# Retention, then a gated feed-forward: where q and k are turned, how the first tails are loaded, and in what pieces the exponents are issued

## The chip, the cores and the metric

The kernel runs on one core of a Trainium2 chip. Five engines work side by side, each through its own list of instructions in order: TensorE (PE in the profile; PEld are its weight loads), VectorE (DVE), ScalarE (ACT), GpSimd (POOL) and SyncE (SP), which here only issues transfers (DMAs). Engines wait for one another by semaphores. The metric is the device time of one execution in microseconds (us). The kernel before took 1175.51 us, the median of three runs (1174.72 to 1177.06).

## The reference

q, k and v are 8 x 8 x 576 x 64 (batch, heads, positions, head size). The feed-forward has 4608 tokens, 512 model columns and 1536 hidden columns. Everything is given as float64 or float32 and computed in float32.

```python
def _attn_ref(q, k, v) -> np.ndarray:
    ...
    scores = scale * np.matmul(q, k.transpose(0, 1, 3, 2))
    gamma = 1.0 - 2.0 ** (-5.0 - np.arange(H, dtype=np.float32))
    ...
    Dmat = np.where(rel >= 0, gamma[:, None, None] ** rel[None, :, :], 0.0)
    ret = scores * Dmat[None, :, :, :]
    return np.matmul(ret, v).astype(np.float32)

def _moe_ref(x, w_gate, w_val, w_out, rms_g) -> np.ndarray:
    rms = np.sqrt(np.mean(x * x, axis=-1, keepdims=True) + 1e-06)
    xn = x / rms * rms_g
    g = xn @ w_gate
    silu = g * (1.0 / (1.0 + np.exp(-g)))
    val = xn @ w_val
    return (silu * val @ w_out).astype(np.float32)
```

The retention's output, heads side by side, is the feed-forward's x.

## The kernel before, in words

**Jobs.** The retention is cut into 32 jobs: one batch and one pair of heads each. A job's 576 positions are nine chunks of 64: four full tiles of 128 positions and a tail of 64. `slot(j)` (line 387) issues on PE the values of job j-1 (L341), then the scores of job j (L270) and the states of its chunks (L290); on DVE it weighs the scores (`ret`, L302), adds the states up (`sums`, L319, with one copy at L317) and multiplies the finished output of job j-1 into x (L380), after PE's carried products (L360). A one-element memset on POOL (`tick`, L349) orders the carried products behind the values.

**Turns.** Scores need q and k with the head size on the partitions. For the first eight jobs `turn(j)` (line 209) does this with PE: 16 records turn_q, 4 turn_k, two for the tails (turn_t, L231) into one bank, and ACT copies them out (L228, L235). From job 8 on, `load_qk` (L142) loads q and k in 32 x 32 blocks into raw tiles, one buffer each, and `prepare(j)` turns them on DVE with two stream transposes (L241) and then scales v on ACT (L250). `following(j)` is `prepare_next(j)`, which prepares job j+1, and `load_next(j)`, which issues the loads of job j+2 on SP.

**Groups of tokens.** The 4608 tokens are 12 groups u of 384. Each has its norm: `norm_0` (squares on ACT, gathered on DVE), `norm_1` (three small products ms on PE, a power on POOL), `diagonals` (DVE, L453) and `norm_2` (a product rb on PE, four scalings of x on DVE, L466, and for u > 1 four differences, L477). Groups 0 and 1 are multiplied plainly: `up_plain` (L554) and `down` (L568). Groups 2 to 11 use seven products instead of eight: in `up(u, m, g)` (m = 0 gate, 1 val; g = 0 to 2) the products come in the order x, y, z, x, w, z, w into four PSUM banks (L497). After y comes the sum u2 = m1 + y on DVE, after z the sum u4 = u2 + z (both named u, L504). The second z product adds into the bank that u4 reads, so it waits for u4; the second w product waits in the same way for the sum c22 (in a gate group `h<-u,w`, in a val group `c<-u,w`). A generator yields after each of the seven. `across(u)` is the same for the output (L627), with 24 records a product. Five banks are shared by all of this. In `up_plain` PE runs ahead until five banks wait for ACT's Silu (L562) or DVE's product (L560).

**Order.** The program is written out by hand and each engine keeps the order of the trace. In the main loop (line 940), after group i of u, `behind(u, i)` puts a slot at certain i (`SLOTS`); it calls `slot(j)`, `prepare_next(j)` and, for i below 5, `load_next(j)`. During u = 2 one step of `combine_out` (DVE, L598) follows each yield.

**Weights.** They come as 64-bit floats in 18 chunks of 1 MB and are rounded on the chip: DVE takes the exponent bits (L745), ACT makes the new exponent in three pieces (L749, L750, L753, 1.15 us each), DVE makes the mantissa (L766, L771), puts in the sign (L775) and joins both (L783). L775 frees the words for the next load, which ACT issues. `weights(n)` issues n steps of this. `combine(m)` makes sums of weight blocks on POOL (L797).

**Start.** `start()` loads the first eight jobs on SP (`load_first`), and the tails of a batch with `load_tails`: all eight heads at once, three loads. Then come the eight jobs, `up_plain` for both groups, `down` for group 1 and for group 0 with slots 8 and 9 between, and the norm of group 2 among the products of `down(0, s)`.

Of the kernel before, what the change touches and what calls it, by code (L numbers as in the profile page):

```python
# [41 lines left out]
def kernel(  # L42
# [101 lines left out]

    def load_first(j):

# [34 lines left out]

    def load_tails(b, queues):


        room = w_up[1][:, 8:].rearrange("p b f -> p (b f)")
        for i, (nm, src) in enumerate((("qt", q), ("kt", k), ("vt", v))):
            t = room[:TAIL, (3 * b + i) * DM : (3 * b + i + 1) * DM]
            t = t.rearrange("p (h d) -> p h d", d=D)
            queues[i].dma_start(out=t, in_=src[b, :, NFULL * P :].rearrange("h p d -> p h d"))
            for hp in range(NHP):  # L190
                st[b * NHP + hp][nm] = t[:, 2 * hp : 2 * hp + 2]
# [17 lines left out]
    def turn(j):  # L209
# [19 lines left out]
        for i, nm in enumerate("qk"):  # L229
# [3 lines left out]
                identity=ident[:TAIL, :TAIL],  # L233
            )
            nc.scalar.copy(out=d[nm + "T"][:, NFULL * P :], in_=last[:, o])  # L235
    def prepare(j):

# [375 lines left out]
    def across(u):  # L613
# [27 lines left out]
        def result(row, col, a, ps):  # L641
            r = ps[:, :U]
            if a is not None:
                r = temp(f"c{row}{col}_{u}")
                add(r, a, ps)
            o = outs.tile([P, DM], F32, tag="o", name=f"o_{u}_{row}_{col}")[:, :U]
            nc.vector.transpose(out=o, in_=r)
            o = o.rearrange("p (d t r) -> p d t r", d=2, r=SQ)
            for d in range(2):
                for i in range(P // SQ):  # L650
                    c0 = row * DH + d * P + i * SQ
                    t0 = u * U + col * HU
                    queue = nc.scalar if u == NU - 1 and d else nc.sync
                    queue.dma_start(
                        out=out[t0 : t0 + HU, c0 : c0 + SQ].rearrange("(t c) r -> c t r", c=SQ),
                        in_=o[i * SQ : i * SQ + SQ, d],
                    )
# [80 lines left out]
    def exponent(i):  # L738

        if i not in words_of:  # L740
# [7 lines left out]
        )  # L748
        nc.scalar.activation(out=e.bitcast(F32), in_=e, func=AF.Relu, bias=least)  # L749
        nc.scalar.activation(  # L750
            out=e.bitcast(F32), in_=e.bitcast(F32), func=AF.Relu, bias=most, scale=-1.0
        )
        nc.scalar.activation(  # L753
            out=e, in_=e.bitcast(F32), func=AF.Relu, bias=top, scale=-(2.0**23)
        )
        exp_of[i] = e

    def mantissa(i):


        if i not in words_of:
# [69 lines left out]
    def start():  # L831
# [10 lines left out]
        nc.scalar.activation(out=tick, in_=mhalf[:1], func=AF.Silu)  # L842
        nc.vector.memset(ones, 1.0)
        first_places.update(find_places())
        for i in (1, 0, 2):
            table(i, nc.scalar)
        for j in range(2 * NHP):
            load_first(j)
            if j == 0:
                load_tails(0, (nc.scalar, nc.scalar, nc.sync))  # L850
            elif j == 1:
                table(3, nc.sync)
            elif j == 3:
                load_tails(1, (nc.sync,) * 3)
            load_chunks((0, 0, 1, 1, 2, 2, 2, 3)[j], nc.sync)
# [7 lines left out]
        for j in range(2 * NHP):  # L863
# [19 lines left out]
        load_kv(2 * NHP)  # L883
        for m, g in [(m, g) for g in range(NG) for m in range(2)]:
            for u in range(2):
                weights_to(4 * g + 2 * m + 1)
                for i, _ in enumerate(up_plain(u, m, g)):
                    if not (u or m or g):
# [98 lines left out]
```

## Time and profile before

| | |
|---|---|
| median of three runs | 1175.51 us |
| the profiled execution, by its own time | 1175.4 us |
| its span, first to last instruction | 1173.6 us |
| PE busy | 1134.3 us (97%) |
| DVE busy | 692.0 us (59%) |
| ACT busy | 248.7 us (21%) |
| bytes moved | 125.37 MB, 107 GB/s on the mean |
| first product of `up_plain` | 68.58 us |
| first product of `down` | 200.15 us |
| first product of `up(2)` | 267.01 us |

The main groups of instructions, from the list by line and shape: count, busy time, mean of one.

| line and what | count | busy us | mean ns |
|---|---|---|---|
| L241 turn of q, 128 x 576, DVE | 24 | 18.5 | 772 |
| L241 turn of k, 128 x 576, DVE | 24 | 17.6 | 735 |
| L504 sum u, 128 x 384, DVE | 120 | 66.0 | 546 to 554 |
| L749, L750, L753 exponent pieces, ACT | 18 each | 20.7 each | 1148 to 1149 |
| L562 Silu of `up_plain`, ACT | 24 | 10.9 | 477 to 484 |
| L235 tail copies, ACT | 16 | 3.4 | 212 to 218 |
| L647 output transposes, 128 x 384, DVE | 40 | 23.2 | 578 to 583 |

How to read it: a busy PE isn't PE at its peak, since ends of products are modelled. A wait is idle time of an engine just before an instruction, put down to what released it last. "issue" is a wait for nothing that the profile shows. Jobs 0 to 7 lie in the first 68 us, the plain products up to 264 us, and the rest repeats with small changes every three groups of tokens.

### The profile page before, as it was taken

The page shows a single profiled execution, that of the slowest core. Times are in us where ns is not written, and L with a number is a line of the kernel's source. Part 1 is how long each engine was busy: PE and PEld are TensorE (multiplying, and loading weights), DVE is VectorE, ACT ScalarE, POOL GpSimd, SP SyncE. Part 2 cuts the span into 40 slices and gives each one's busy share as a digit, 9 for nine tenths or more (in the row PEclk, how much of TensorE's full clock was granted, in tenths as well). Part 3 has the DMA queues.
Part 4 walks back from the last instruction along what each step waited for, and adds up shares of the span by engine and source line. Part 5 has one row for each costly group of instructions (what it writes and reads, how often), then busy time and mean ns, then how long its engine had stood idle before and what let it go on. Part 6 is the DMA issues. An engine that isn't in the chain of part 4 may idle for free.

```text
span 1173.6 us, 24291 instructions
## 1 busy us (share of the span) xinstructions
PE 1134.3 (97%) x10320; PEld 1024.2 (87%) x10320; DVE 692.0 (59%) x1410; ACT 248.7 (21%) x484; POOL 46.4 (4%) x74
## 2 busy tenths in 40 slices
PE   6689999998999999999999999999999999999998
PEld 5655555448999999999999999999999999999998
DVE  4688874018766675465675676356567566446352
ACT  5446641102111120121120211120220110120110
POOL 0000005410000000000000000000000000000000
PEclk9899999999999999999999999999999999999999
DMA  9744421422764546216426356306435412403304
GB/s 213 223 112 143 140 75 48 135 58 50 235 150 58 136 128 113 107 55 129 114 67 120 96 133 135 122 2 138 101 98 130 110 58 88 129 1 94 122 1 108
DMA packets 282364, 125.37 MB, mean 107 GB/s; under 512 B 257168, under 2 KB 264848, under 8 KB 282256
## 3 DMA queue, kind: packets, MB, share of 16 engines
q1 hardware_dynamic: 271584, 108.45, 37.2%
q10 hardware_dynamic: 10672, 15.38, 4.1%
q8 instruction: 81, 1.33, 0.5%
q14 instruction: 27, 0.22, 0.1%
HBM read 108.83 MB, written 14.94 MB: 105 GB/s over the span
## 4 chain that ended last, share of the span: by engine, by line
PE 83%; DVE 12%; issue 2%; DMA 2%; ACT 1%; DVEq 0%; SPq 0%; POOL 0%; POOLq 0%; ACTq 0%
PE z L497 12%; PE w L497 12%; PE x L497 10%; PE up L554 8%; PE xo L627 7%; PE wo L627 7%; PE zo L627 7%; PE out L568 5%; PE y L497 5%; PE yo L627 3%; DVE sum L319 3%; DVE x L380 2%; PE av L341 2%; PE s L270 2%; PE s L290 1%
## 5 line engine op out<-in xcount | busy, mean ns | idle before, releaser
L521 ACT COPY m<-x 128x384 f32<-128x384 f32 x60 | 28.8, 479 | 419.0 <-PE x L497 394.2
L497 PE MATMUL z<-x,w_gate 128*128 128x192 f32 x480 | 88.6, 328 | 6.6 <-DVE u L504 5.3
L497 PE MATMUL z<-x,w_val 128*128 128x192 f32 x480 | 88.6, 328 | 3.3 <-DVE u L504 3.3
L497 PE MATMUL x<-x,w_val 128*128 128x192 f32 x480 | 88.8, 328 | 0.0
L497 PE MATMUL x<-x,w_gate 128*128 128x192 f32 x480 | 88.5, 328 | 0.0
L497 PE MATMUL w<-sums,w_val 128*128 128x192 f32 x480 | 87.8, 326 | 0.0
L497 PE MATMUL w<-sums,w_gate 128*128 128x192 f32 x480 | 87.8, 326 | 0.0
L497 PEld LDWEIGHTS z<-x,w_gate 128*128 128x128 f32 x480 | 79.2, 190 | 8.9 <-DVE u L504 7.4
L497 PEld LDWEIGHTS z<-x,w_val 128*128 128x128 f32 x480 | 79.2, 190 | 5.7 <-DVE u L504 5.7
L627 PE MATMUL xo<-h,w_out 128*128 128x192 f32 x480 | 82.1, 328 | 0.0
L627 PE MATMUL wo<-h,w_out 128*128 128x192 f32 x480 | 81.3, 326 | 0.0
L497 PEld LDWEIGHTS x<-x,w_val 128*128 128x128 f32 x480 | 79.2, 190 | 0.6
L497 PEld LDWEIGHTS x<-x,w_gate 128*128 128x128 f32 x480 | 79.3, 190 | 0.5
L497 PEld LDWEIGHTS w<-sums,w_val 128*128 128x128 f32 x480 | 79.6, 190 | 0.0
L497 PEld LDWEIGHTS w<-sums,w_gate 128*128 128x128 f32 x480 | 79.6, 190 | 0.0
L627 PEld LDWEIGHTS xo<-h,w_out 128*128 128x128 f32 x480 | 78.1, 190 | 0.5
L627 PEld LDWEIGHTS wo<-h,w_out 128*128 128x128 f32 x480 | 78.5, 190 | 0.0
L504 DVE TENSOR_TENSOR u<-m,y 128x384 f32<-128x384 f32 x60 | 32.7, 546 | 77.5 <-PE y L497 77.5
L504 DVE TENSOR_TENSOR h<-u,w 128x384 f32<-128x384 f32 x60 | 33.2, 554 | 69.3 <-PE w L497 68.7
L302 DVE SCALAR_TENSOR_TENSOR ret<-s,causal 128x320 f32<-128x320 f32 x64 | 28.4, 484 | 67.6 <-PE last L290 41.7
L516 ACT ACTIVATE h<-h 128x384 f32<-128x384 f32 x90 | 47.1, 523 | 95.8 <-DVE h L504 95.8
L554 PE MATMUL up<-x,w_val 128*128 128x384 f32 x192 | 62.7, 487 | 2.4 <-ACT w_val L562 2.4
(151 smaller groups left out, 1779.2 us busy)
## 6 DMA issues: line engine op xcount, KB each, us to landing
w_out<-w_blocks SPq DMA_DIRECT2D x70, 768.0 KB, 5.3
out_dram<-o SPq DMA_DIRECT2D x304, 24.0 KB, 1.6
qraw<-in_q_dram SPq DMA_DIRECT2D x96, 72.0 KB, 2.6
kraw<-in_k_dram SPq DMA_DIRECT2D x96, 72.0 KB, 2.6
k<-in_k_dram SPq DMA_DIRECT2D x48, 128.0 KB, 3.0
v<-in_v_dram SPq DMA_DIRECT2D x48, 128.0 KB, 3.4
w_blocks<-w_out SPq DMA_DIRECT2D x7, 768.0 KB, 7.0
w_out<-in_moe_w_gate_dram ACTq DMA_DIRECT2D x4, 1024.0 KB, 5.2
```

Source lines behind the costliest of these rows:

```text
L270: nc.tensor.matmul(s[side(odd), e, i * L : i * L + L], lhsT=d["kT"][side(e), c * L : c * L + L], rhs=d["qT"][side(e), c * L : c * L + L], ...
L302: nc.vector.scalar_tensor_tensor(out=ret[:, e], in0=s[:, e, :SC].rearrange("p (c k) -> p c k", k=L), scalar=float(_gamma(H)[2 * hp + e] ** ...
L319: nc.vector.scalar_tensor_tensor(out=t[:, c], in0=t[:, c - 1], scalar=gc[:, hp : hp + 1], in1=part, op0=ALU.mult, op1=ALU.add,)
L341: mm = nc.tensor.matmul(av[odd][column(j, odd, e), i * L : i * L + L], lhsT=d["v"][side(odd), i, e] if c < NC - 1 else d["vt"][:, e], rhs= ...
L380: nc.vector.tensor_tensor(out=x[to, first - c0 // L :: 2], in0=av[odd][at, i * L : (i + n) * L].rearrange("p (c k) -> p c k", k=L), in1=g. ...
L497: nc.tensor.matmul(ps[:, i * HU : i * HU + HU], lhsT=w_up[m][:, 2 * blk + c, cut], rhs=t_of[u][blk][:, c], start=(start and i == c == 0), ...
L504: nc.vector.tensor_tensor(out=o, in0=a, in1=pairs_of(ps), op=ALU.add)
L516: nc.scalar.activation(out=o, in_=c, func=AF.Silu)
L521: nc.scalar.copy(out=s1, in_=pairs_of(x_))
L554: nc.tensor.matmul(ps[:, :U], lhsT=w_up[m][:, 4 * half + c, i * P : i * P + P], rhs=x_of[u][:, c], start=(c == 0), stop=(c == NHP - 1),)
L568: nc.tensor.matmul(ps[:, :DM], lhsT=h_of[u][:, f, s * P : s * P + P], rhs=w_out[:, f], start=(f == 0), stop=(f == NF - 1),)
L627: nc.tensor.matmul(ps[:, i * HU : i * HU + HU], lhsT=w_slots[:, k % 4, c, i * P : i * P + P], rhs=rhs[:, c], start=(start and i == c == 0) ...
```

## The change

- `load_tails` loads the tails of some heads only, one of q, k, v at a call, always on SP. For batch 0 the tails of heads 0 and 1 follow k and v of job 0, and those of heads 2 to 7 follow k and v of job 1; for batch 1 all eight heads follow k and v of job 4 (before, they came after job 3).
- `turn` issues both tail transposes, then both copies.
- Six products of a tile of ones into a bank of their own are issued on PE at the start.
- The three ACT pieces of an exponent go into a list `acts`; `act(1)` issues one of them at given points, and `act(chunk=i)` the rest of a chunk before L775 needs it.
- In the first jobs the last gather of group 0, its diagonals and its norm_2 are issued earlier; the norm of group 2 moves from `down(0, s)` to `down(1, s)`.
- `behind` no longer calls `prepare_next(j)`; it notes j in `turns`, and the turn is issued after the third yield of the next `up` (behind u2 and u4), or in `across` after its first product. `load_next(j)` stays where it was.
- In the last group of tokens each output transpose is done in two halves, and stores alternate between SP and ACT.

```diff
-    def load_first(j):
+    def load_first(j, tails):
...
+            for n in (0, 1) if nm == "k" else (2,):
+                load_tails(b, n, tails)
...
-    def load_tails(b, queues):
+    def load_tails(b, n, heads):
...
+        if heads:
+            room = w_up[1][:, 8:].rearrange("p b f -> p (b f)")
+            nm, src = (("qt", q), ("kt", k), ("vt", v))[n]
...
+            cut = slice(heads[0], heads[-1] + 1)
+            nc.sync.dma_start(
+                out=t[:, cut], in_=src[b, cut, NFULL * P :].rearrange("h p d -> p h d")
+            )
...
                 identity=ident[:TAIL, :TAIL],
             )
+        for i, nm in enumerate("qk"):
+            o = slice(i * TAIL, i * TAIL + TAIL)
             nc.scalar.copy(out=d[nm + "T"][:, NFULL * P :], in_=last[:, o])
...
+                if end:
+                    half = slice(d * HU, d * HU + HU)
+                    nc.vector.transpose(out=o[:, half], in_=r[:, half])
                 for i in range(P // SQ):
...
-                    queue = nc.scalar if u == NU - 1 and d else nc.sync
+                    queue = nc.scalar if end and i % 2 else nc.sync
...
+        f = e.bitcast(F32)
+        acts.extend((
+            (i, dict(out=f, in_=e, bias=least)), (i, dict(out=f, in_=f, bias=most, scale=-1.0)),
+            (i, dict(out=e, in_=f, bias=top, scale=-(2.0**23))),
+        ))
         exp_of[i] = e
+
+    acts = []
+
+    def act(n=0, chunk=-1):
+
+        while acts and (n > 0 or acts[0][0] <= chunk):
+            nc.scalar.activation(func=AF.Relu, **acts.pop(0)[1])
+            n -= 1
...
         yield
+        act(chunk=i)
         nc.vector.scalar_tensor_tensor(
             out=e, in0=hi, scalar=0x80000000, in1=e, op0=ALU.bitwise_and, op1=ALU.bitwise_or
         )
...
+        warm = bank("warm")
+        for _ in range(6):
+            nc.tensor.matmul(warm[:, :P], lhsT=ones, rhs=ones, start=True, stop=True)
...
-            load_first(j)
-            if j == 0:
-                load_tails(0, (nc.scalar, nc.scalar, nc.sync))
-            elif j == 1:
+            load_first(j, {0: range(2), 1: range(2, H), NHP: range(H)}.get(j))
+            if j == 1:
                 table(3, nc.sync)
-            elif j == 3:
-                load_tails(1, (nc.sync,) * 3)
...
+            act(1)
             if j == 5:
                 norm_1(0)
             elif j == 6:
+                norm_2(0)
+            weights((0, 1, 2, 2, 2, 2, 0, 0)[j])
+            if j == 4:
+                gather(*squares.pop())
+            elif j == 5:
                 diagonals(0)
-            weights((0, 1, 2, 2, 2, 2, 0, 0)[j])
-            if j == 6:
-                norm_2(0)
+            act(1)
...
                     weights(2)
+                    act(1)
                     if i == 1:
...
-                if u == 0:
+                if u == 1:
                     (norm_0, norm_1, norm_2)[s](2)
...
+    turns = []
+
     def behind(u, i):
...
             slot(j)
-            prepare_next(j)
+            turns.append(j)
...
-                for _ in up(u, i % 2, i // 2):
+                for n, _ in enumerate(up(u, i % 2, i // 2)):
                     next(made, None)
+                    if n == 2 and turns:
+                        prepare_next(turns.pop())
...
             for i, _ in enumerate(rest):
+                if i == 0 and turns:
+                    prepare_next(turns.pop())
```

More of the change, by code (lines that the diff above doesn't have):

```diff
@@ L180, in find_places @@
         }
-    def load_tails(b, queues):
-        room = w_up[1][:, 8:].rearrange("p b f -> p (b f)")
-        for i, (nm, src) in enumerate((("qt", q), ("kt", k), ("vt", v))):
-            t = room[:TAIL, (3 * b + i) * DM : (3 * b + i + 1) * DM]
-            t = t.rearrange("p (h d) -> p h d", d=D)
-            queues[i].dma_start(out=t, in_=src[b, :, NFULL * P :].rearrange("h p d -> p h d"))
-            for hp in range(NHP):
+    def load_tails(b, n, heads):
+        if heads:
+            room = w_up[1][:, 8:].rearrange("p b f -> p (b f)")
+            nm, src = (("qt", q), ("kt", k), ("vt", v))[n]
+            t = room[:TAIL, (3 * b + n) * DM : (3 * b + n + 1) * DM]
+            t = t.rearrange("p (h d) -> p h d", d=D)
+            cut = slice(heads[0], heads[-1] + 1)
+            nc.sync.dma_start(
+                out=t[:, cut], in_=src[b, cut, NFULL * P :].rearrange("h p d -> p h d")
+            )
+            for hp in range(heads[0] // 2, heads[-1] // 2 + 1):
                 st[b * NHP + hp][nm] = t[:, 2 * hp : 2 * hp + 2]
@@ L646, in result @@
             o = outs.tile([P, DM], F32, tag="o", name=f"o_{u}_{row}_{col}")[:, :U]
-            nc.vector.transpose(out=o, in_=r)
-            o = o.rearrange("p (d t r) -> p d t r", d=2, r=SQ)
+            end = u == NU - 1
+            if not end:
+                nc.vector.transpose(out=o, in_=r)
+            o_of = o.rearrange("p (d t r) -> p d t r", d=2, r=SQ)
             for d in range(2):
+                if end:
+                    half = slice(d * HU, d * HU + HU)
+                    nc.vector.transpose(out=o[:, half], in_=r[:, half])
                 for i in range(P // SQ):
@@ L652, in result @@
                     t0 = u * U + col * HU
-                    queue = nc.scalar if u == NU - 1 and d else nc.sync
+                    queue = nc.scalar if end and i % 2 else nc.sync
                     queue.dma_start(
                         out=out[t0 : t0 + HU, c0 : c0 + SQ].rearrange("(t c) r -> c t r", c=SQ),
-                        in_=o[i * SQ : i * SQ + SQ, d],
+                        in_=o_of[i * SQ : i * SQ + SQ, d],
                     )
@@ L748, in exponent @@
         )
[L749 to L755, printed above, removed]
-        exp_of[i] = e
+        f = e.bitcast(F32)
[3 more added lines that the diff above has]
+        ))
+        exp_of[i] = e
+    acts = []
[3 more added lines that the diff above has]
+            n -= 1
     def mantissa(i):
```

## The prediction

> **What bounds the kernel now.** First the page's header and its slices: TensorE (PE) is busy almost everywhere, and only the first three slices (29.3 us each), the tenth and the last are below nine tenths. The transfers are dense only in the first two.
>
> ```profile
> span 1173.6 us, 24291 instructions
> ...
> PE   6689999998999999999999999999999999999998
> ...
> DVE  4688874018766675465675676356567566446352
> ...
> DMA  9744421422764546216426356306435412403304
> ```
>
> So a gain must come out of PE's gaps: 1173.6 - 1134.3 = 39.3 us in all. The second view, what PE waited for (total, times, longest), names them:
>
> ```profile
> PE z L497 <- DVE u L504: 8.6, 15, 1.6
> PE s L290 <- issue: 4.6, 1, 4.6
> PE turn_q L223 <- DMA h<-in_q_dram: 3.9, 1, 3.9
> PE up L554 <- ACT w_val L562: 2.4, 1, 2.4
> PE av L360 <- issue: 2.3, 1, 2.3
> PE turn_t L231 <- ACT qT L235: 2.2, 5, 0.6
> PE turn_t L231 <- DMA w_val<-in_k_dram: 2.1, 1, 2.1
> PE turn_t L231 <- ACT qT L228: 1.9, 3, 1.6
> PE rb L464 <- DVE diag L453: 1.2, 1, 1.2
> PE z L497 <- DVE x L380: 1.2, 1, 1.2
> ```
>
> Third, the timeline of one slot in the steady part (start, us, engine). VectorE (DVE) turns q and k between the slot's sums and the sums u of the next group. The second z product must wait for the last u: PE's product before it began at 380.43, products stand 1.30 us apart, so z was due at 381.73.
>
> ```profile
> 379.73 0.77 DVE L241 STREAM_TRANSPOSE qT<-qraw 128x576 f32<-128x576 f32 x1
> ...
> 380.42 0.73 DVE L241 STREAM_TRANSPOSE kT<-kraw 128x576 f32<-128x576 f32 x1
> 380.43 1.46 PE L497 MATMUL w<-sums,w_val 128*128 128x192 f32 x8
> ...
> 381.08 0.52 DVE L504 TENSOR_TENSOR u<-m,y 128x384 f32<-128x384 f32 x1
> 381.70 0.56 DVE L504 TENSOR_TENSOR u<-u,z 128x384 f32<-128x384 f32 x1
> ...
> 382.31 1.57 PE L497 MATMUL z<-x,w_val 128*128 128x192 f32 x8 [0.41 <-DVE u L504]
> ```
>
> Last, windows over the first jobs (stretch, length, busy PE, weight loads, DVE, ACT, POOL, granted clock, DMA share, GB/s). Transfers fill the DMA engines, PE stands still for instructions from 45.2 to 49.8, and the clock falls to about 0.6 after each pause.
>
> ```profile
> 30.00:34.00 4.00, 4.00 (x102) 3.78 (x94) 2.37 (x8) 0.85 (x3) 0.00 (x0) 0.61 1.16 324
> ...
> 46.00:50.00 4.00, 0.18 (x12) 0.18 (x15) 0.00 (x0) 0.00 (x0) 0.00 (x0) 1.00 1.08 364
> 50.00:54.00 4.00, 4.00 (x67) 3.68 (x64) 3.37 (x13) 0.12 (x1) 0.00 (x0) 0.57 0.31 115
> ```
>
> **What the skill says.** "TensorE: Matmul & The Clock Gate", Part 1, says that the array runs at half clock until about 3.4 us of activity, and falls back after a pause. The trace agrees in effect: 16 turn_q records took 1.98 us at 12.64 and 1.09 us at 19.35, though its clock column shows 1.00 at both. The same page (Architectural detail) calls ScalarE (ACT) and DVE strict first-in first-out. The trace agrees: at 183.19 ACT's exponent had waited 8.0 us for DVE, and Silus of finished products stood behind it. "DMA: Bandwidth & Descriptors", Issuing engines are not separate DMA queues, says that loads from any queue share 16 engines. So moving the tails from ACT to SP moves issue time, not bandwidth; the share of 1.0 in the first 20 us fits. "Runtime: NRT & Kernel Launch", Instruction fetch mechanics, says that crossing a 256-instruction block is mostly hidden; here it isn't: 253 records ran from 40.4 to 45.2 between two stalls of 2.3 and 4.6 us.
>
> **The turns.** Twenty-one turns are deferred. Seven fall into the output products, 3.90 us each, where PE shows no wait: nothing gained or lost. Fourteen fall into an up group. Nothing leaves DVE: the turn (1.35 us of DVE's time) changes places with two u sums. Then z is free in time, and the next to be late is the second w product, which needs the sum c22 (`h<-u,w` or `c<-u,w`). That sum comes after the same set of work as before, so its end is unchanged. In a val group (8 of the 14) it ended at 383.18; w was due at 383.03 and started at 383.71. It can start at about 383.3: 0.4 us each, 3.2 in all. In a gate group (5) c22 ended at 572.83 against a due time of 572.82, before it w started at 573.63: 0.7 each, 3.5. The group at 299 also carries the steps of combine_out between the sums, c22 ends at 300.6 and w started at 300.79: 0.1. Sum 6.8. Bounds: all that is lost there now, 5 x 0.8 + 8 x 0.68 + 1.3 = 10.7 with restarts; 3.5 if only the gate groups gain. The four scalings of v on ACT (about 1.7 us) move between the copy m and the Silu; the 3.4 us that ACT idles there cover them. SP's loads of the next q and k (4 + 4 issues, 4.1 us, landing 2.6 us later) and of k, v, vt behind them wait for the turn, which ends about 1.2 us later. The tightest place is after the turn at 422.38: its reload of k is issued until 427.3, lands near 429.9, and the next turn comes at 436.55, 6.6 us later, and itself moves back; elsewhere over 10 us are left. Behind the loads on SP stand only weight fetches and stores.
>
> **Norm of group 2, earlier.** Before up(2), DVE does four scalings (2.20 us) and four differences (2.26) while PE wants the slot's and the group's sums: PE is busy 19.82 of 23 us in 267 to 290. Moved under down(1, .), all of it (squares on ACT, 3 ms products, POOL's power, diagonals) lies beside 31 us of PE work in which DVE is busy 2.45 of 33 us. The POOL power stands behind combine(0), which ended at 204.75, well before it is asked for at about 221; combine(1) behind it starts some 5 us later and was over at 234.9, 45 us before its use. What is late next: slot 9's turn, which is not deferred, as at 299 (1.0 us idle). So 3.2 idle become about 1.1, with 0.3 for restarts: 2.4. Bounds 1.3 and 3.3.
>
> **Exponents one at a time.** At 184.8 PE had filled its five banks, because two Silus waited at 186.62 behind three exponent pieces (3 x 1.15). With one piece between two Silus, the Silu starts when the first piece ends, 184.36: the 2.4 us go. DVE's L775 waits for the third piece up to 1 us longer; its product is needed at 200, ten us later. Bounds 1 and 2.4 us.
>
> **The first jobs.** The first tail k load (512 pieces, 4.5 us) held scores(0) to 10.17. With two heads' tails instead, and both tail transposes before their copies, the turn of job 0 could end near 7.2. But v of job 0 is now issued behind two more loads (about 0.6 us each, the price of a 32 KB vt load) and a wait, lands near 8.5, and takes 1.7 us to scale: states(0) start near 10.0, not 11.19: 1.2 us. The six warm products (12 records, about 1.5 us cold) run before 3.87, where PE waits for q anyway: at no cost there; they save anything from nothing to 3 us, as the clock may rise a few us sooner. Job 3: qT waits behind three exponents until 27.41, PE idles 1.56 and then runs 4 us at 0.61. Together 3.1. The tail copies: five waits of 0.4, of which I count 1.0 (the rest is DVE's). The norm of group 0: the diagonal is ready, 1.2, and 62 to 66 at 0.73 cost 1.1. Sum 7.6. Against it: v of jobs 3, 4 and 5 landed within about 0.5 us of its scaling (v of job 4 issued until 25.2 with 4.4 us to land, scaled at 29.05), and SP issues five loads more ahead of job 2 (2.7 us). What PE gains before 37 us is therefore partly given back to transfers and to the two instruction stalls, while jobs 6 and 7 have 4 and 8 us of slack. I take 6. Bounds: 10 (both stalls and all clock loss gone) and 0 (bound by transfers, stalls longer).
>
> **The end.** The last transpose is cut in two (0.39 us a half, from 0.58 for 384 and 0.77 for 576 columns), so the first stores start at 1169.46, not 1169.68. Each queue still has four issues (1.8 us): 0.2.
>
> **Sum.** 6.8 + 2.4 + 2.4 + 6.0 + 0.2 = 17.8 us. The profiled execution took 1175.4 us (its span of 1173.6 and 1.8 around it), almost the median of 1175.5. That gives **1157.6 us**.
>
> **Rivals.** (1) The start stays bound by transfers and instruction fetch, and val groups gain nothing: 0 + 3.6 + 2.4 + 2.4 + 0.2 = 8.6, hence 1166.8. For it: a DMA share of 0.76 to 1.31 in all windows from 8 to 50 us. Against it: jobs 6 and 7, and the waits on ACT and DVE, which are no transfers. Chance 0.25. (2) Slower: DVE stops at a deferred turn because its raw tile isn't there (q and k have one raw buffer, and its reload waits for this very turn), with five sums queued behind it and PE out of banks. Each us counts once per group. It decides from 0.8 us per group, (17.8 - 6.8) / 14, beyond what is lost now. At 1.5 us: 14 x 1.5 = 21 against 11 gained, so 1185.4. Against it stand the margins above. Chance 0.08. (3) The deferred turns don't move, because the loads traced ahead of them force the old order: 1175.4 - 11.0 = 1164.4. Chance 0.06, taken with the first.
>
> **How the numbers follow.** The forecast has 0.58, rivals 1 and 3 together 0.31, the slower one 0.08, no change 0.03. Faster by over 0.2% (what a measurement of this kernel can tell, 2.4 us): 0.89; within: 0.03; slower: 0.08. The forecast's own range is 1152 to 1163; with the bounds (low: 10 + 9 + 3.3 + 2.4 + 0.5 = 25.2, 1150.2; high: rival 1 and a little more) 1150 to 1168.
>
> **What would show it.** Right: no `z <- u` waits, at most 0.3 us at w in their place; z of up(2) waiting 1 us at most; no wait of up on the Silu; up's first product near 62 instead of 68.58. Wrong: waits of DVE on qraw or kraw, w waits over 0.8 us, or stalls of "issue" above 7 us in all before 70 us.

## The result, and the profile after

The kernel after takes 1155.86 us (median of 4 runs, 1155.05 to 1157.02); the kernel before, beside it, 1175.28 us (4 runs). The ratio is 0.9833, with a 95% interval of 0.9816 to 0.985: 19.6 us less, between 17.6 and 21.6. The profiled execution took 1157.02 us, its span is 1155.2 us.

The page of the kernel after, header and slices:

```profile
span 1155.2 us, 24332 instructions
...
PE   7899999999999999999999999999999999999998
...
DVE  3888864428676575465765775465576566445352
...
DMA  7945322322972656034345456306336403303304
```

Only two slices at the start and the last one are below nine tenths now; the dent in the tenth slice is gone. What PE waited for (total, times, longest), to be read against the list of the kernel before:

```profile
PE av L351 <- ACT qT L235: 3.4, 1, 3.4
PE s L280 <- ACT kT L235: 2.3, 2, 1.9
PE turn_t L238 <- ACT qT L235: 1.5, 3, 0.7
PE warm L868 <- DVE ones L865: 1.2, 1, 1.2
PE s L280 <- issue: 1.1, 2, 0.7
PE z L507 <- DVE u L514: 1.0, 1, 1.0
PE rb L474 <- DVE sum L329: 1.0, 1, 1.0
PE w L507 <- DVE h L514: 0.8, 1, 0.8
```

(Lines have moved by some ten: L507 is the old L497, L280 the old L270, L351 the old L341.) The 8.6 us of `z <- u` are down to one wait of 1.0, the wait of up for the Silu is no longer there, and the two stalls of "issue", 6.9 us, are short ones now. The first two lines are new.

The group with a deferred turn, in the timeline of the kernel after (start, us, engine):

```profile
366.69 1.46 PE L507 MATMUL x<-x,w_val 128*128 128x192 f32 x8
...
367.94 0.55 DVE L514 TENSOR_TENSOR u<-u,z 128x384 f32<-128x384 f32 x1
...
367.99 1.46 PE L507 MATMUL w<-sums,w_val 128*128 128x192 f32 x8
368.41 0.77 DVE L251 STREAM_TRANSPOSE qT<-qraw 128x576 f32<-128x576 f32 x1
369.11 0.73 DVE L251 STREAM_TRANSPOSE kT<-kraw 128x576 f32<-128x576 f32 x1
...
369.29 1.46 PE L507 MATMUL z<-x,w_val 128*128 128x192 f32 x8
...
370.21 0.54 DVE L514 TENSOR_TENSOR c<-u,w 128x384 f32<-128x384 f32 x1
...
370.80 1.57 PE L507 MATMUL w<-sums,w_val 128*128 128x192 f32 x8
```

Both u sums now end before the turn begins, and z starts 1.30 us after w, on time. The next w, due at 370.59, starts at 370.80 because c22 ends at 370.75: the 0.2 us that remain are at the place the prediction named.

Where the time went shows best by stages, whose limits are rows of the PE timelines. "First" is a product's start, the stages are differences (us). The upper rows are the two kernels, the others are the experiments below.

| kernel | first up | up to first down product | to first xo of u = 2 | to the end of the span |
|---|---|---|---|---|
| before | 68.58 | 131.6 | 134.8 | 838.6 |
| after | 62.39 | 128.9 | 131.3 | 832.7 |
| turns | 65.48 | 131.4 | 134.2 | 832.6 |
| norm | 67.70 | 131.1 | 132.2 | 838.7 |
| acts | 62.99 | 129.5 | 134.8 | 838.7 |
| acts_up | 68.56 | 129.5 | 134.8 | 838.6 |
| first | 68.64 | 131.4 | 134.8 | 839.1 |
| no_first | 63.31 | 129.3 | 131.3 | 832.5 |
| no_warm | 64.82 | 129.1 | 131.2 | 832.7 |
| short_warm | 61.26 | 128.9 | 131.2 | 832.7 |

So the 18.4 us of the spans are 6.2 in the first jobs, 2.7 in the plain up part, 3.5 up to u = 2's output and 5.9 after it.

But the first jobs have new waits too. The timeline there, ACT and PE:

```profile
13.02 0.51 ACT L260 ACTIVATE first_sums<-first_sums,gv 128x256 f32<-128x256 f32 x1 [4.15 <-DMA first_sums<-in_v_dram]
...
14.58 0.56 ACT L235 COPY qT<-turn_q 128x512 f32<-128x512 f32 x1
...
15.20 1.01 PE L351 MATMUL av<-ret,first_sums 64*64 64x64 f32 x26 [3.42 <-ACT qT L235]
```

Job 1's scaling of v stands ahead of job 1's turn copies on ACT. It waited 4.15 us for a v that SP issued at 8.79, behind the new tail loads, where before it did so at 7.27. The turned q and k lay ready in PSUM meanwhile, and av waited until their copy had freed its place.

### The profile page after: what moved, and what is told of

The parts are those of the page before. It is cut to its first block, busy times and chain, and to the rows that moved or that the text cites. A ratio compares the mean times of both kernels' runs of the same rounds, so it can differ in the third digit from the quotient of the medians.

```text
span 1155.2 us, 24332 instructions
## 1 busy us (share of the span) xinstructions
PE 1132.9 (98%) x10332; PEld 1025.7 (89%) x10332; DVE 696.4 (60%) x1414; ACT 246.4 (21%) x484; POOL 46.5 (4%) x74
## 3 DMA queue, kind: packets, MB, share of 16 engines
q8 instruction: 81, 1.33, 0.5%
## 4 chain that ended last, share of the span: by engine, by line
PE 91%; DVE 4%; SPq 2%; issue 1%; ACT 1%; DMA 1%; DVEq 0%; POOL 0%; POOLq 0%
PE w L507 13%; PE x L507 13%; PE z L507 13%; PE up L564 11%; PE xo L637 7%; PE wo L637 7%; PE zo L637 7%; PE y L507 6%; PE out L578 5%; PE yo L637 3%; PE av L351 2%; PE s L280 1%; PE s L300 1%; PE av L370 1%; SPq L161 1%; DVE sum L329 1%
## 5 line engine op out<-in xcount | busy, mean ns | idle before, releaser
L507 PE MATMUL w<-sums,w_val 128*128 128x192 f32 x480 | 88.6, 328 | 0.4
L507 PE MATMUL z<-x,w_gate 128*128 128x192 f32 x480 | 87.9, 326 | 1.0 <-DVE u L514 1.0
L507 PE MATMUL w<-sums,w_gate 128*128 128x192 f32 x480 | 88.0, 326 | 0.8 <-DVE h L514 0.8
L507 PE MATMUL x<-x,w_val 128*128 128x192 f32 x480 | 88.7, 328 | 0.0
L507 PE MATMUL x<-x,w_gate 128*128 128x192 f32 x480 | 88.5, 328 | 0.0
L507 PE MATMUL z<-x,w_val 128*128 128x192 f32 x480 | 87.8, 326 | 0.0
L507 PEld LDWEIGHTS w<-sums,w_val 128*128 128x128 f32 x480 | 79.2, 190 | 2.7 <-DVE c L514 2.7
L507 PEld LDWEIGHTS z<-x,w_gate 128*128 128x128 f32 x480 | 79.6, 190 | 1.3 <-DVE u L514 1.3
L507 PEld LDWEIGHTS w<-sums,w_gate 128*128 128x128 f32 x480 | 79.4, 190 | 1.3 <-DVE h L514 1.1
L507 PEld LDWEIGHTS x<-x,w_val 128*128 128x128 f32 x480 | 79.2, 190 | 0.6
L507 PEld LDWEIGHTS x<-x,w_gate 128*128 128x128 f32 x480 | 79.3, 190 | 0.5
L507 PEld LDWEIGHTS z<-x,w_val 128*128 128x128 f32 x480 | 79.6, 190 | 0.0
L564 PE MATMUL up<-x,w_gate 128*128 128x384 f32 x192 | 63.3, 488 | 0.9 <-DVE x L476 0.7
```

What stands on the lines that cost most here:

```text
L507: nc.tensor.matmul(ps[:, i * HU : i * HU + HU], lhsT=w_up[m][:, 2 * blk + c, cut], rhs=t_of[u][blk][:, c], start=(start and i == c == 0), ...
L564: nc.tensor.matmul(ps[:, :U], lhsT=w_up[m][:, 4 * half + c, i * P : i * P + P], rhs=x_of[u][:, c], start=(c == 0), stop=(c == NHP - 1),)
```

## Experiments: each part alone

Theory: the parts lie in different stages, so each is worth what its own waits were, and they add up. Rivals: the waits only move (turns, norm); the start is bound by transfers, so nothing that is done there counts.

The kernel before was run again beside each experiment; its medians there are 1175.8 to 1177.0 us. Each ratio is taken from all runs of the two kernels side by side and is not the quotient of the two medians; a gain in us below is (1 - ratio) times 1175.3. The stages come from one profiled execution each.

**turns**: the kernel before with the deferred turns alone.

```diff
-            prepare_next(j)
+            turns.append(j)
...
-                for _ in up(u, i % 2, i // 2):
+                for n, _ in enumerate(up(u, i % 2, i // 2)):
                     next(made, None)
+                    if n == 2 and turns:
+                        prepare_next(turns.pop())
...
             for i, _ in enumerate(rest):
+                if i == 0 and turns:
+                    prepare_next(turns.pop())
```

> The kernel before with the deferred turns alone. Theory (parts are separate, each worth what its own waits were): 6.5 us faster than before, near 1168.8, because fourteen up groups lose their z wait (0.66 on average) without a new wait at w; the output groups gain nothing; no z wait above 0.3 us after 300. Rival A (val groups gain nothing, w is late instead): 3.5 us faster, near 1171.8, with w waits of 0.5 us or more in val groups. Rival B (the turn is not the cause, the order of the sums is forced elsewhere): no change, z waits as before. First up product stays at 68.6 in both.

Measured: 1170.58 us, ratio 0.9934 (0.9916 to 0.9952), or 7.8 us (5.6 to 9.9). The stages put 6.0 us after u = 2 and 0.6 into u = 2. From 300 us on, the list of waits of PE has one line left (before: 6.0 us of `z <- u` in 13 waits, and this line):

```profile
PE av L360 <- POOL tick L349: 0.3, 1, 0.3
```

Both rivals fall. That its first up product came 3.1 us early although nothing was changed there is chance (the profiled execution, 1165.45 us, is the fastest of its six); see the instruction stalls below.

**norm**: the kernel before with one line changed, `if u == 0:` to `if u == 1:` at the norm of group 2.

> The kernel before with the norm of group 2 under the first output group alone. Theory: 2.4 us faster (1172.9), waits in 267 to 290 shrink from 3.2 to about 1.1 us, the output products of 200 to 267 unchanged. Rival (the norm's four scalings and differences displace DVE work under down that PE then waits for, or the slot behind it is late): less than 1 us, with new waits of s or ret between 230 and 260.

Measured: 1174.35 us, ratio 0.9973 (0.996 to 0.9986), or 3.2 us (1.6 to 4.7). The stage that holds it is 2.6 us shorter, and the one behind it stands (838.7 against 838.6). PE's waits from 267 to 290 us, 3.2 us in before, are down to one of z, 0.98 us. No wait of s or ret came up. The rival falls.

**acts** and **acts_up**: the exponents piece by piece; in acts everywhere, in acts_up in the plain up part alone.

```diff
-        nc.scalar.activation(out=e.bitcast(F32), in_=e, func=AF.Relu, bias=least)
...
+        acts.extend((
+            (i, dict(out=f, in_=e, bias=least)), (i, dict(out=f, in_=f, bias=most, scale=-1.0)),
+            (i, dict(out=e, in_=f, bias=top, scale=-(2.0**23))),
+        ))
         exp_of[i] = e
+        if not pieces:
+            act(3)
...
         gather(*squares.pop())
+        pieces.append(1)
         load_qk(2 * NHP)
```

The last three added lines are those of acts_up; acts has, in their place, the `act(1)` of the change behind the square and behind the weights of each first job.

> The kernel before with the exponents issued piece by piece alone (in the first jobs and in the plain up part). Theory: 2.4 us at the Silu of 184 to 187 and 1 to 3 us in the first jobs (the pause of job 3 and the slow clock after it): 3.4 to 5.4 us faster, near 1171. Rival (the first jobs are bound by transfers and instruction blocks, so only the Silu counts): 2.4 us faster, near 1172.9, first up product at 68.6 as before.

> The kernel before with the exponents issued piece by piece in the plain up part only; in the first jobs all three pieces follow each other as before. Theory (of the 8.5 us that all the pieces gave, 2.2 are the Silu's wait and the rest is made in the first jobs): 2.2 us faster than before, near 1173.5; first up product at 65.5 to 68.6, no wait of up on the Silu at 187. Rival (the pieces in the first jobs gave nothing and the earlier first up product of those runs was chance): 6 us or more faster.

Measured: acts 1168.49 us, ratio 0.9927 (0.9911 to 0.9942), or 8.6 us (6.8 to 10.5): more than either side had expected. acts_up 1173.8 us, ratio 0.9979 (0.9969 to 0.9989), or 2.5 us (1.3 to 3.6), with the up stage 2.1 us shorter and no Silu wait. The difference, 0.0052 or 6.1 us (about 4 to 8), is made by the pieces in the first jobs: 68.56 against 62.99 at the first up product.

**first**: the kernel before with the smaller tail loads on SP and both tails turned before their copies, without the warm products, exponents and norm as before.

```diff
-            load_first(j)
-            if j == 0:
-                load_tails(0, (nc.scalar, nc.scalar, nc.sync))
-            elif j == 1:
+            load_first(j, {0: range(2), 1: range(2, H), NHP: range(H)}.get(j))
+            if j == 1:
                 table(3, nc.sync)
-            elif j == 3:
-                load_tails(1, (nc.sync,) * 3)
```

> The kernel before with the smaller tail loads (all on SP, heads 0 and 1 first) and both tails turned before their copies; no warm products, the exponents and the norm of group 0 as before. Theory (job 0 earlier, later jobs give part of it back to v landing late): first scores before 8, a new wait near 15 for v of job 1, first up product 1 to 3 us earlier than 68.6, total 1 to 3 us faster. Rival A (it is the loads alone that make the start shorter): first up product near 63, 5 to 6 us faster. Rival B (transfer bound, tails in front of job 1 cost as much as they save): within 1 us of before.

Measured: 1177.02 us, ratio 0.9991 (0.9979 to 1.0002): 1.1 us, between 2.5 faster and 0.2 slower, which is rival B or the low end of the theory. The scores of job 0 do start at 7.62 instead of 10.17, and the first up product comes at 68.64, as before. Its waits show what took it back:

```profile
PE z L506 <- DVE u L513: 8.3, 14, 1.6
PE s L299 <- issue: 4.1, 1, 4.1
PE av L350 <- ACT qT L235: 4.1, 2, 2.1
```

The third line stands for two waits. The one of 2.0 us at 15.57 is the scaling of v ahead of the copies. In front of the one of 2.1 at 31.39 stood a scaling that waited 3.36 us for v, and behind it three exponents in a row, from 27.37 on, which the whole change issues one at a time; so the tails may be worth more in the whole change than alone. The second line is an instruction stall as before.

**no_first**: turns, norm and acts together, without the tail loads, the turn of both tails, the warm products, the earlier norm of group 0 and the halved last transpose.

> Deferred turns, norm of group 2 moved and exponents piece by piece, without the smaller tail loads, the turn of both tails at once, the warm products, the earlier norm of group 0 and the halved last transpose. Theory (the exponents alone made the start shorter, the tails are worth nothing): as fast as the whole change, 1155 to 1158, first up product at 62 to 64. Rival (the tails, warm products and norm of group 0 carry 3 us or more of the start once the exponents are out of the way): 1159 to 1162, first up product at 65 or later.

Measured: 1158.36 us (1156.7 to 1160.05), ratio 0.985 (0.9833 to 0.9867), or 17.6 us; first up product at 63.31. The three parts alone sum to 7.8 + 3.2 + 8.6 = 19.6, inside the interval of 15.6 to 19.6 at its edge. What it leaves out is worth 2.0 us by the ratios (2.5 by the medians), and the intervals overlap, so that it isn't told from nothing: between the theory and the rival, nearer the theory.

## Experiments: why the first jobs became shorter

In acts no transfer is moved in the program, and PE has the same instructions in the same order, so the gain of 5.6 us by the first up product can be followed from instruction to instruction. Job 3's wait of 1.56 us is gone, but in its place job 4's turn waits for ACT:

```profile
34.97 0.27 PE L231 MATMUL turn_t<-ident,w_val 64*128 64x64 f32 x1 [2.83 <-ACT qT L228]
...
45.81 0.39 PE L290 MATMUL s<-w_val,first_v 64*64 64x64 f32 x11 [0.96 <-issue]
...
46.10 1.11 PE L360 MATMUL av<-qT,sum 64*64 64x64 f32 x32
47.14 1.09 PE L223 MATMUL turn_q<-ident,h 128*64 128x128 f32 x16
```

That put acts 1.4 us behind (the carried products of L360 began at 38.77, in before at 37.35), and it caught up because the first instruction stall, 2.27 us at 40.41 in before, is missing. At 45 us acts is thus hardly ahead: the eleven records of `s` begin their stall at 44.85, those of the kernel before at 45.25, 0.4 us later. Then 3.6 us of the gain are the second stall's length, 0.96 against 4.57 us, and 1.6 us the pace of the two groups of products behind it, 1.96 and 1.85 us against 1.11 and 1.09. Together these are the 5.6. In the kernel before:

```profile
44.80 0.45 PE L290 MATMUL s<-w_val,first_v 64*64 64x64 f32 x14
49.82 0.39 PE L290 MATMUL s<-w_val,first_v 64*64 64x64 f32 x11 [4.57 <-issue]
...
50.10 1.96 PE L360 MATMUL av<-qT,sum 64*64 64x64 f32 x32
51.99 1.85 PE L223 MATMUL turn_q<-ident,h 128*64 128x128 f32 x16
```

Instructions come in packets of a queue of their own, among the data. In the view of the transfers from 47.0 to 47.5 us of the kernel before (queue, packets, MB, share of 16 engines):

```profile
DMA packets 148, 0.20 MB, mean 400 GB/s; under 512 B 42, under 2 KB 73, under 8 KB 147
...
q1 hardware_dynamic: 147, 0.18, 101.8%
q8 instruction: 1, 0.02, 12.8%
```

and from 43.0 to 43.5 us of acts:

```profile
DMA packets 455, 0.16 MB, mean 325 GB/s; under 512 B 410, under 2 KB 454, under 8 KB 454
...
q1 hardware_dynamic: 454, 0.15, 117.8%
q8 instruction: 1, 0.02, 15.8%
```

The page of the kernel before counts 81 packets of q8, 1.33 MB in all. PE and PEld have 20640 instructions, so one packet (0.02 MB) fits one block of about 255 of TensorE's instructions. In windows of half a microsecond, for all kernels in which this stall is at these same eleven records (the block that ends there begins with the records behind the first stall; in acts, which has no such stall, its begin is an estimate, 18 records into the group of 32 that starts at 38.77; the third weight chunk is a load of 1 MB that SP, in late_chunks ACT, issues near it):

| kernel | pieces in the first jobs | block begins | third chunk issued | q8 packet in | PE goes on at | stall |
|---|---|---|---|---|---|---|
| before | no | 40.41 | 40.65 | 47.0-47.5 | 49.82 | 4.57 |
| turns | no | 39.86 | 41.89 | 44.0-44.5 | 46.80 | 2.10 |
| norm | no | 39.18 | 39.22 | 46.5-47.0 | 49.65 | 4.84 |
| acts_up | no | 40.69 | 40.42 | 47.5-48.0 | 49.94 | 4.30 |
| first | no | 42.84 | 44.13 | 48.0-48.5 | 50.97 | 4.09 |
| late_chunks | no | 40.43 | 36.68 | 50.0-50.5 | 52.64 | 4.35 |
| acts | yes | 39.6 (estimate) | 41.94 | 43.0-43.5 | 45.81 | 0.96 |
| no_first | yes | 38.98 | 42.54 | 43.0-43.5 | 45.97 | 2.15 |
| no_warm | yes | 39.30 | 42.16 | 44.5-45.0 | 46.83 | 2.22 |

PE goes on some 2 to 3 us after the packet in every row, so the stall is a late packet. Before, turns, norm and acts_up are alike up to here, and their stalls still range from 2.1 to 4.8 us: a single profile of this start is uncertain by some 3 us. Over the rows, though, the stalls are 4.0 us on average without the pieces and 1.8 with them.

The third chunk sorts the rows better than the pieces do. Where it was issued before the block began or within 0.3 us of it (before, norm, acts_up, late_chunks), the packet passed 6.6 to 10.1 us after that begin; where it came 1.3 to 3.6 us behind it (the other five, turns among them), 3.4 to 5.7 us. This fits an instruction packet held up by data ahead of it: with the pieces SP issued this load at 41.9 to 42.5, in before at 40.65, although its line was not moved. But it is read from one profile of each kernel, and no run moved this load alone, so it isn't shown to be the cause.

**late_chunks** was to ask whether the weight chunks delay the packet.

```diff
-            load_chunks((0, 0, 1, 1, 2, 2, 2, 3)[j], nc.sync)
+            load_chunks((0, 0, 1, 1, 2, 2, 2, 2)[j], nc.sync)
...
-        load_chunks(4, nc.sync)
         turn(0)
...
+            if j > 5:
+                load_chunks(j - 3)
             if j:
                 u, c = divmod(j - 1, NHP)
```

> The kernel before with the loads of the weight chunks 3 and 4 (1 MB each) issued on ACT in the loop of jobs 6 and 7 instead of on SP with the jobs' loads. Theory (TensorE's instruction packets come late behind data packets; the second instruction stall ended about 2.5 us after its packet, and the packet came 4.4 to 6.8 us after the block before it began): with less data in flight at 40 to 50 us the second stall falls from 2.1 to 4.8 us to at most 1 us, first up product 2 to 4 us earlier, 2 to 4 us faster. Rival (q, k and v of the last jobs already fill the queues, chunks 3 and 4 come after the stall): stall and time unchanged within 1 us.

Measured: 1181.03 us, ratio 1.0034 (1.0021 to 1.0047), 4.0 us slower, and the stall stays (4.35). Neither theory nor rival expected that, and the theory wasn't put to the test, because the edit did not defer the loads: the rounding steps of jobs 2 to 5 ask for chunks five ahead and now found chunks 3 and 4 still to be issued, so ACT issued them itself at 36.68 and 37.50, and the chunk that it had issued at 37.25 followed at 40.92. The timeline of ACT:

```profile
36.68 0.40 ACTq L729 DMA_DIRECT2D w_out<-in_moe_w_val_dram  x1
...
37.50 0.41 ACTq L729 DMA_DIRECT2D w_gate<-in_moe_w_val_dram  x1
...
40.92 0.37 ACTq L729 DMA_DIRECT2D w_out<-in_moe_w_gate_dram  x1
41.34 1.15 ACT L749 ACTIVATE w_gate<-w_gate,least 128x1024 f32<-128x1024 uint32 x1 [2.77 <-DVE sum L319]
```

The three exponents behind it began at 41.34 instead of 37.85, the next turn copies stood behind them, and PE waited 3.1 us for ACT. So this run doesn't tell which data the packet waits for. It did the opposite of what was meant: both chunks went out earlier than in before (40.65 and 45.98), and the packet came later than in any other row. It shows again what three exponents in a row cost when a job's copies come due.

**no_warm** and **short_warm**: the kernel after without the six warm products, and with one column instead of 128 in each.

```diff
-            nc.tensor.matmul(warm[:, :P], lhsT=ones, rhs=ones, start=True, stop=True)
+            nc.tensor.matmul(warm[:, :1], lhsT=ones, rhs=ones[:, :1], start=True, stop=True)
```

> The kernel after without the six warm products. Theory (turn_q runs at 1.98 us for 16 records with and without them, and TensorE waits for v of job 1 at 15 us anyway): within 1 us of after, 1155 to 1157; turn_k and the first scores at about 1.35 instead of 0.8 us, the wait at 15 us shorter by as much. Rival (the early clock carries through the first jobs): 2 us or more slower than after, first up product at 64 or later.

> The kernel after with the six warm products cut to one column each: as many instructions ahead of the first turn, so the 256-instruction blocks end at the same places, but about 0.8 us of work instead of 2.9. Theory (the warm products are worth 2 to 3 us because they shift the places where TensorE waits for its next instructions): as after, 1155 to 1157, the instruction pauses at the same instructions as there, turn_k and first scores back at about 1.1 and 0.8 to 1.35. Rival (they are worth it through the clock, 7 to 10 us at full speed instead of half): as without them, 1158.5 to 1160.5, although the pauses stay where after has them.

Measured: no_warm 1159.64 us (1156.78 to 1162.01), ratio 0.9856 (0.9837 to 0.9876); short_warm 1156.53 us (1155.84 to 1158.12), ratio 0.9842 (0.9829 to 0.9856); after 0.9833 (0.9816 to 0.985). By the ratios the six products are worth 2.7 us (3.8 by the medians), against my expectation of under 1, and the short ones 1.6 (3.1); the three intervals overlap, so that neither is told from nothing. What the traces do show is that the earlier pace of after is lost again by 15 us. PE's timeline of after:

```profile
5.96 0.79 PE L224 MATMUL turn_k<-ident,first_k 128*128 128x128 f32 x4
...
15.20 1.01 PE L351 MATMUL av<-ret,first_sums 64*64 64x64 f32 x26 [3.42 <-ACT qT L235]
```

and of short_warm:

```profile
5.80 1.12 PE L224 MATMUL turn_k<-ident,first_k 128*128 128x128 f32 x4
...
15.38 1.01 PE L351 MATMUL av<-ret,first_sums 64*64 64x64 f32 x26 [3.08 <-ACT qT L235]
...
40.41 1.02 PE L370 MATMUL av<-qT,sum 64*64 64x64 f32 x26 [3.24 <-issue]
```

In short_warm turn_k took 1.12 us, as without warm products, and both kernels then wait for v of job 1 at 15 us. (The short products spanned 2.7 us, not the 0.8 that I expected, and the long ones 2.9; the two kernels differ less in this time than in the pace of turn_k behind it.) With twelve records more in front, the pauses for instructions fall on other records than in no_warm, as the theory says; but they aren't always shorter, as the 3.24 at 40.41 shows, where after has none. If the products are worth anything, shifted block ends are the explanation that is left; they aren't shown to be the cause.

## Experiments: a faster version

**scale_later** takes up the new wait at 15 us: v of a job is scaled behind the same job's copies.

```diff
         scale_v(0)
-        scale_v(1)
...
                 turn(j + 1)
+                scale_v(j + 1)
             if squares:
                 gather(*squares.pop())
-            if j + 2 < 2 * NHP:
-                scale_v(j + 2)
```

**sums_first** takes up z at 265.9 and w at 289.0, **best2** does both in a milder form.

```diff
         slot(9)
-        following(9)
+        turns.append(9)
+        load_next(9)
...
-                    next(made, None)
+                    if n not in (1, 2):
+                        next(made, None)
```

In best2 the last two lines are `for _ in range((2, 0, 0, 0, 2, 2, 2)[n]): next(made, None)`.

> The kernel after with v of a job scaled on ACT after the turn copies of the same job instead of one job ahead. Theory (the copies of job 1 stood 3.4 us, those of job 4 1.9 us, behind a scaling that waited for v): both waits go, first up product 2 to 4 us earlier than 62.4, total 2 to 4 us faster than after, near 1152. Rival A (the states then wait for the scaling, 1.7 us a job, which values and scores do not cover): waits of s on ACT in several jobs, no gain or slower. Rival B (the freed time goes to instruction stalls): no gain, longer stalls of issue.

> The kernel after with the turn of slot 9 deferred into the first group of u = 2 too, and the 24 differences of w_out spread over four or five groups and kept from between the u sums. Theory: the waits of z at 265.9 (1.0) and w at 289.0 (0.8) go, 1.5 to 2 us faster than after, near 1154. Rival (the differences then come late for across, or the turn is late for slot 10): xo of u = 2 waits on SP's fetch or DVE, no gain.

> The kernel after with v of a job scaled behind the turn copies of the same job, the turn of slot 9 deferred into the first group of u = 2, and two of the 24 differences of w_out at a time issued after the copy m and after c22, done in the fourth group as before. Theory: no wait of xo on the fetch (8.9 us when the differences ended in the fifth group), z at 266 and w at 289 together 1.8 shorter, the start 0 to 1.5 us shorter: 1 to 3 us faster than after, 1153 to 1155. Rival (two differences at a time make the slot's sums late instead): waits of w or x on DVE of 1 us or more between 266 and 300, no gain.

Measured: scale_later 1155.4 us, ratio 0.982 (0.9804 to 0.9836); sums_first 1168.54 us, ratio 0.9931 (0.9917 to 0.9946); best2 1155.2 us, ratio 0.9819 (0.9801 to 0.9837).

In scale_later the two waits are gone and the first up product comes at 60.87, 1.5 us earlier than in after; a stall of 3.43 us for instructions at 37.83 and waits of s for the scaling (1.4 us in three) took the rest, so that both rivals hold in part. sums_first does remove z's wait, but gave back far more; its list of waits begins

```profile
PE xo L637 <- DMA w_out<-w_blocks: 8.9, 1, 8.9
```

The differences end two groups later, SP can fetch the blocks of w_out only from 324.26 instead of 304.88, and the output products wait for them: the rival's case. best2 keeps the old end of the differences and has no such wait; in u = 2 the timeline of PE has

```profile
264.94 1.57 PE L507 MATMUL w<-sums,w_gate 128*128 128x192 f32 x8 [0.22 <-DVE h L514]
280.94 1.54 PE L507 MATMUL z<-x,w_gate 128*128 128x192 f32 x8 [0.29 <-DVE x L390]
285.72 1.57 PE L507 MATMUL z<-x,w_gate 128*128 128x192 f32 x8 [0.65 <-DVE u L514]
287.51 1.57 PE L507 MATMUL w<-sums,w_gate 128*128 128x192 f32 x8 [0.22 <-DVE h L514]
```

1.4 us in four waits for 1.8 in two, and the stage is 131.7 against 131.3 us: nothing won. Neither of the two quicker kernels is told from after by its interval.

## Why the prediction was right, point by point

The forecast of 17.8 us met 19.6 (17.6 to 21.6). Term by term:

- **Turns, 6.8.** Right in size and in mechanism: 6.6 us by the stages of turns, 7.8 (5.6 to 9.9) by its time. The next to be late is w, by 0.2 us, behind c22, as worked out (0.3). In one group it was more: w waits 0.85 us at 288.97, which by the letter is over the 0.8 that the prediction named as a sign of being wrong. It is the group (299 in before) in which the steps of combine_out stand between the sums; there z had waited 1.01 us, so its gain is near the 0.1 that was counted. The loads that the later turn pushes back cost nothing: no turn is listed as waiting for its raw tile (an output's transpose is, once, 1.5 us beside a load of kraw, with no wait of PE behind it), so rival 2 had no place to start from, and rival 3 falls with turns.
- **Norm of group 2, 2.4.** Right: 2.6 by its stage, 3.2 (1.6 to 4.7) by time. Slot 9's turn is what is late next, with 0.97 us at 265.91 (predicted 1.1). One reading was off, with nothing hanging on it: combine(1) was over at 237.6 in before, not at 234.9.
- **The Silu, 2.4.** Right: 2.1 by its stage, 2.5 (1.3 to 3.6) by time.
- **The first jobs, 6.0.** The sum was right (6.2 at the first up product), its terms were not, so that the hit is in part luck. Job 3's exponents, put at 3.1, measured 6.1 (about 4 to 8), and not by the way that was worked out: the wait went from job 3 to job 4 and grew from 1.56 to 2.83 us, and the gain came from the instruction stalls and the slow products behind them. The step that failed is the one that gave part of the gain back "to the two instruction stalls": I took them for fixed, and they shrank, from 6.84 us in before to 0.96 in acts and 2.96 in no_first. Job 0's tails, 1.2, and the tail copies, 1.0, together measured 1.1 (-0.2 to 2.5): job 0 gained as said, states(0) even more (8.68 in after, not 10.0), and v of job 1, for which I took 0.6 us a load on SP but no wait, came late and held ACT. The two errors had opposite signs. The norm of group 0 was not run alone.
- **Warm products, "anything from nothing to 3 us"**: 2.7 by the ratios of no_warm and after (3.8 by the medians), with overlapping intervals; I had given them no term. They spanned 2.9 us, not about 1.5, and held turn_q back by 0.2 (4.05 against 3.87), which is not quite "at no cost".
- **The end, 0.2.** Not seen: the last stage is 832.7 with the halved transpose and 832.5 to 832.6 without it.

Rival 1 is half right where it says that the start is bound by transfers and instruction fetch: the tails alone gave next to nothing. It erred in taking every edit there for a transfer's shadow; an edit on ACT alone gave 6.1 us. Its other half, val groups that gain nothing, falls with the stage of 832.6. The evidence for it was a little too smooth, too: from 20 to 24 us the DMA share was 0.55. And the forecast's lowest bound takes 9 us for the turns, though their own bound is 10.7.

What stays open: why the instruction packet comes earlier with the pieces. No line that issues a transfer was moved in acts, and late_chunks didn't do what it should have. It may be the time between block ends, or data in front of the packet. The issue time of the third chunk speaks for the second, but no run decides it.

## What to carry to other kernels

Sum a change by stages, not over the whole kernel: turns, norm and acts_up each showed up in the stages that they change and left the later stages within 0.5 us, while chance moved the start by 3 us. Cut a row of long ACT steps into pieces between which short copies that free PSUM for TensorE can pass (8.6 us here). Put nothing that waits for a transfer in front of such copies either; here that was worth 1.5 us at the first up product of one profile (scale_later), too little to be seen in the whole. Where a start is dense in transfers, a load that is moved ahead makes another one late: look for the one that it passes before counting the gain.

## What the hardware showed that I had not expected

- TensorE went on 1.8 to 3.2 us after the packet with its next instructions had passed, in nine kernels of nine. Under a DMA share near 1.0 (1.08 from 46 to 50 us of before) the packet was late enough to stall it by 1.0 to 4.8 us, and the same code gave 2.1 and 4.8. "Runtime: NRT & Kernel Launch", Instruction fetch mechanics, calls such crossings mostly hidden; in this start the measurement decides otherwise, while over the whole kernel it fits (81 packets, and two waits of "issue" in the list of before).
- Such a stall can cost more than its length. The 48 records behind it took 3.8 us in before (stall 4.57) and 3.5 in turns (2.10), but 2.2 in acts (0.96) and in no_first (2.15), so that the length alone doesn't decide it.
- Six fp32 products of one column each (12 records) spanned 2.7 us at the start, those of 128 columns 2.9 us; yet only behind the long ones was turn_k at 0.79 us, against 1.12.
